# Idle matmuls, scalings and state copies in the first chunks of a fused retention and feed-forward kernel

## The chip, the cores and the metric

The kernel runs on one core of a Trainium2 chip. The metric is the device time of one execution in microseconds (us); lower is better. PE is the matmul engine, PEld its weight loads, DVE the vector engine, ACT the scalar engine, POOL GpSimd, and SP the engine whose queue issues most DMAs.

## The reference

Four sequences of 768 tokens go through a linear attention with a decaying state (8 heads of 64), and the result, seen as 3072 tokens of width 512, through a feed-forward layer with a squared ReLU.

```
def _attn_ref(q, k, v):                       # q, k, v: (4, 8, 768, 64) float32
    gamma = 1.0 - 2.0 ** (-5.0 - np.arange(H))
    scale = 1.0 / np.sqrt(D)
    for t in range(S):
        state = gamma * state + einsum('bhd,bhe->bhde', k[:, :, t], v[:, :, t])
        y[:, :, t] = scale * einsum('bhd,bhde->bhe', q[:, :, t], state)

def _moe_ref(x, w_in, w_out):                 # x: (3072, 512), w_in: (512, 2048)
    h = np.maximum(x @ w_in, 0.0)
    return h * h @ w_out
```

## The kernel before

The tokens are taken in 24 chunks of 128, six for each sequence. Within a chunk the attention is done by matmuls: q and k are scaled by powers of gamma (so that the decay is in the operands), both are transposed on PE, the scores of the chunk are a product of kT and qT, a mask makes them causal, and the output is the masked scores times v plus qT times the state of the chunks before. The state is a sum of products of k and v that grows in one PSUM tile, `c_ps`; after each chunk it is copied to SBUF in bf16, into one of the tiles `s_bd`, whose off-diagonal quarters stay zero. The output of a chunk, `y`, is copied into `xt`, which is the transposed input of the feed-forward part.

The feed-forward part runs over 11 blocks of tokens, the first of four chunks, the others of two. Its first product, with `w_in` (four groups of 512 columns, each loaded in float32 to a `stage` tile and cast to bf16 by `cast_w`), is made by `first_product` at L824; ACT takes the ReLU and DVE or ACT the square. The second product with `w_out` is made at L1020 for the first two blocks and by a scheme of seven products at L858 for the others. From the first block on, a table of places puts the attention of later chunks between pieces of the feed-forward part.

There is no scheduler: every engine runs its instructions in the order in which the Python code gives them out, and each queue is in order. SP issues the loads in the order of the code at the start: the first half of q of chunks 0 to 3, half of k of chunks 0 and 1, the second half of q, the second half of k, k of chunks 2 and 3, v of chunks 0 and 1, the first half of `w_in` group 0, v of chunks 2 and 3, and then the other groups of `w_in`. POOL issues the loads of `w_out` (L170) after its casts of `w_in`.

The change touches the front, which is the hand-written order for chunks 0 to 3 before the table of places begins. Chunks go in pairs there, (0, 1) and (2, 3), and heads in two groups of four; a tile holds one group:

- `scale_q4(group, rr)` (L533) scales half of the q of four chunks for one group of heads, on DVE unless told otherwise; `transpose_q4` (L550) turns it by four matmuls and ACT copies it to `qT` (L553).
- `scale_pair_k(m, group)` (L559) and `transpose_pair_k` (L584, copy to `kT` by ACT at L585) do so for k of the pair that begins with chunk m.
- `cast_pair_v(m, r)` casts half of a pair's v to bf16, on POOL (L571) or ACT (L569).
- `scores_pair(m, group, ...)` (L600) makes 32 small score matmuls of 64 by 64, four of them on different quarters of the array, and then two masks on DVE (L608). "Scores (0, 1)" is this for pair 0 and group 1.
- `state_pair(m, j)` adds chunk m+j to the state by eight matmuls with 64 of 128 rows (L625) and copies the two halves of the state to `s_bd`, by ACT (L636) or by DVE (L638).
- `outputs_pair` (L649) makes the masked scores times v, `finish_pair` (L665) adds qT times the state and copies the result to `xt` by ACT (L677) or DVE (L679).
- `first_unit(0, 0, c, parts)` makes first products of chunk c with `w_in` group 0, in halves of two row blocks.
- `keep_awake(n, width)` issues n matmuls of the identity with itself (L342), 512 columns wide unless told otherwise, into a PSUM tile that nobody reads; the tile comes from the pool of `y`. `end_awake` gives the tile up.

The engines are named by the helpers' arguments: `nc.gpsimd` is POOL, the default is DVE.

Of the kernel before, what the change touches and what calls it, by code (L numbers as in the profile page):

```python
# [31 lines left out]
def kernel(  # L32
# [9 lines left out]
    nc = tc.nc  # L42
    P = nc.NUM_PARTITIONS

    B, H, S, D = q.shape
    DM, DFF = moe_w_in.shape
    C = 128
# [289 lines left out]
    def keep_awake(n, width=4 * C, pool=ps_f, name="psf"):  # L337
        if not idle_ps:
            idle_ps.append(pool.tile([P, 4, P], FP32, name=name))
        wide = max(1, width // C)  # L340
        for _ in range(n):
            nc.tensor.matmul(  # L342
                idle_ps[0][:, 0:wide, 0 : width // wide],
                lhsT=ident[:],
                rhs=ident[:, None, 0 : width // wide].to_broadcast([P, wide, width // wide]),
                start=True,
                stop=True,
            )

    def end_awake():  # L350
        idle_ps.clear()
# [170 lines left out]
    def pair_view(t):  # L522
        return t.rearrange("s c hh d -> s (c hh d)").rearrange("s (r h d) -> s r h d", r=2, h=H)
# [3 lines left out]
    def scale_q4(group, rr, engine=nc.vector):  # L527
        if rr == 0:
            t = qspool.tile([P, 2, H, D], BF16, name="qs").rearrange("s r h d -> s (r h d)")
            qs4[group] = t.rearrange("s (r h d) -> s r h d", h=H // 2, r=4)  # L530
        rs = slice(2 * rr, 2 * rr + 2)
        heads = heads_of[group]
        engine.tensor_tensor(  # L533
            out=qs4[group][:, rs].rearrange("s r h d -> s h r d"),
            in0=raw_q4[group][:, :, rs, :],
            in1=qf4[:, rs, heads]
            .rearrange("s r h -> s h r")[:, :, :, None]
            .to_broadcast([P, H // 2, 2, D]),
            op=ALU.mult,
        )  # L540

    def transpose_q4(group, rr, pool, name):
        if rr == 0:
            t = qTpool.tile([P, 2, NPAIR, C], BF16, name="qT").rearrange("e r p s -> e (r p s)")
            qT4[group] = t.rearrange("e (r p s) -> e r p s", r=4, p=2)
        tp = pool.tile([P, 2, NPAIR, C], BF16, name=name)[:, 0]
        tp = tp.rearrange("e (r p) s -> e r p s", r=2)
        for r in range(2):
            for p in range(2):
                nc.tensor.transpose(  # L550
                    tp[:, r, p, :], qs4[group][:, 2 * rr + r, 2 * p : 2 * p + 2, :], ident[:]
                )
        nc.scalar.activation(qT4[group][:, 2 * rr : 2 * rr + 2], tp, AF.Copy)  # L553

    def scale_pair_k(m, group, engine=nc.vector):
        b, i = chunks[m]
        heads = heads_of[group]
        at[m]["ks"] = pair_view(ks_bd2s[m // 2])
        engine.tensor_tensor(  # L559
            out=at[m]["ks"][:, :, heads],  # L560
            in0=raw_k[m][:, :, heads],
            in1=kfp[:, i : i + 2, heads, None].to_broadcast([P, 2, H // 2, D]),
            op=ALU.mult,
        )

    def cast_pair_v(m, r, on_scalar=False):
        at[m]["v"] = pair_view(v_bd2s[m // 2])
        if on_scalar:
            nc.scalar.activation(at[m]["v"][:, r], raw_v[m][:, r], AF.Copy)  # L569
        else:  # L570
            nc.gpsimd.tensor_copy(at[m]["v"][:, r], raw_v[m][:, r])  # L571

    def transpose_pair_k(m, group, pool, name):
        a = at[m]
        if "kT" not in a:
            a["kT"] = kTpool.tile([P, 2 * NPAIR, C], BF16, name="kT").rearrange(
                "e (r p) s -> e r p s", r=2
            )
        tp = pool.tile([P, 2, NPAIR, C], BF16, name=name)[:, 0]
        tp = tp.rearrange("e (r p) s -> e r p s", r=2)  # L580
        for r in range(2):
            for p in range(2):
                h = 4 * group + 2 * p
                nc.tensor.transpose(tp[:, r, p, :], a["ks"][:, r, h : h + 2, :], ident[:])  # L584
        nc.scalar.activation(a["kT"][:, :, 2 * group : 2 * group + 2], tp, AF.Copy)  # L585

    def tokens_of(m, group, p, j):
        s0 = (m + j) * (C // 4)
        return qT4[group][:, :, p, s0 : s0 + C // 4]

    def scores_pair(m, group, pools, pt):
        a = at[m]
        sts = [pool.tile([P, 2, 2, C], FP32, name=name) for pool, name in pools]
        pt = pt.rearrange("s (hh r p t) -> s hh r p t", hh=2, r=2, p=2)
        a["pt", group] = pt
        for r in range(2):
            for p in range(2):
                for hh, head in enumerate(halves):
                    for j, rows in enumerate(halves):
                        nc.tensor.matmul(  # L600
                            sts[hh][rows, r, p, :],
                            lhsT=a["kT"][head, r, 2 * group + p, j * (C // 2) : (j + 1) * (C // 2)],
                            rhs=tokens_of(m, group, p, j)[head],
                            start=True,
                            stop=True,
                        )
        for hh in range(2):
            nc.vector.tensor_tensor(  # L608
                out=pt[:, hh],
                in0=sts[hh][:],  # L610
                in1=maskp.rearrange("s r q t -> s r (q t)")[:, :, None, :].to_broadcast(
                    [P, 2, 2, C]
                ),
                op=ALU.mult,
            )

    def state_pair(m, j, on_scalar=True):
        b, i = chunks[m]
        a = at[m]
        if i + j == 0:  # L620
            c_ps[0] = ps_c.tile([P, NPAIR, 2, D], FP32, name="c_ps")
        c = c_ps[0]
        for p in range(NPAIR):
            for r in range(2):
                nc.tensor.matmul(  # L625
                    c[:, p],
                    lhsT=a["ks"][halves[j], r, 2 * p : 2 * p + 2, :],
                    rhs=a["v"][halves[j], r, 2 * p : 2 * p + 2, :],
                    start=(i + j == 0 and p == 0 and r == 0),
                    stop=True,  # L630
                    skip_group_check=True,
                )
        s_bd = s_bds[(m + j) % 2]
        for hh, head in enumerate(halves):
            if on_scalar:
                nc.scalar.activation(s_bd[head, :, hh, :], c[head, :, hh, :], AF.Copy)  # L636
            else:
                nc.vector.tensor_copy(s_bd[head, :, hh, :], c[head, :, hh, :])  # L638
# [407 lines left out]
    tp, st, f = (ps_tp, "tp"), (ps_st, "st"), (ps_f, "psf")  # L1046
    def small_pt():
        return ptpool.tile([P, NPAIR, 2, C], BF16, name="pt").rearrange("s p hh t -> s (p hh t)")

    spare = hpool.tile([P, 4096], BF16, name="h2")  # L1050
    keep_awake(6, pool=ps_y, name="y")
    scale_q4(0, 0)
    scale_q4(0, 1)
    transpose_q4(0, 0, *tp)
    transpose_q4(0, 1, *st)
    scale_pair_k(0, 0)
    transpose_pair_k(0, 0, *f)
    keep_awake(1, C)
    scale_q4(1, 0)
    scale_q4(1, 1, nc.gpsimd)  # L1060
    scale_pair_k(0, 1)
    transpose_q4(1, 0, *f)
    scores_pair(0, 0, (st, f), small_pt())
    transpose_pair_k(0, 1, *f)
    transpose_q4(1, 1, *f)
    scale_pair_k(2, 0)
    scale_pair_k(2, 1, nc.gpsimd)
    keep_awake(1)
    scores_pair(0, 1, (tp, f), small_pt())
    transpose_pair_k(2, 0, ps_c, "c_ps")  # L1070
    cast_pair_v(0, 0)
    cast_pair_v(0, 1, on_scalar=True)
    transpose_pair_k(2, 1, *f)
    scores_pair(2, 0, (st, f), spare[:, 0:1024])
    end_awake()
    state_pair(0, 0)
    scores_pair(2, 1, (tp, f), spare[:, 1024:2048])
    outputs_pair(0, 0, ((ps_y, "y"), f))
    outputs_pair(0, 1)
    finish_pair(0, 0)  # L1080
    finish_pair(0, 1)
    state_pair(0, 1)
    cast_w("in", 0, (0,), "GGGG")
    cast_pair_v(2, 0)
# [4 lines left out]
    outputs_pair(2, 0, ((ps_y, "y"), st))  # L1089
    outputs_pair(2, 1)  # L1090
    finish_pair(2, 0)
    state_pair(2, 0, on_scalar=False)
    first_unit(0, 0, 0, (1,))
    first_unit(0, 0, 1, (1,))
    finish_pair(2, 1, on_scalar=False)
# [136 lines left out]
```

## Time and profile before

| | us |
|---|---|
| three runs | 207.69, 208.91, 208.88 |
| median | 208.88 |
| profiled execution | 208.75 |
| its span, first to last instruction | 206.7 |
| PE busy in the span | 198.4 |
| DVE, ACT, POOL busy | 152.1, 128.5, 66.8 |
| mean granted clock of PE | 0.975 |

The profile is of one execution. Its page gives for each engine the busy time, the share of the span and the instructions; then the span in 40 slices of 5.17 us with a digit for the busy tenths of each engine, and in the row PEclk the clock that PE was granted, in tenths of the full one (9 stands for nine tenths or more). A row of the timeline gives the start, the busy time, the engine, the line of the kernel, the operation, what is written and read, the shape and the count, and in brackets how long the engine had been idle and what ended that.

### The profile page before, as it was taken

The page shows a single profiled execution, that of the slowest core. Times are in us where ns is not written, and L with a number is a line of the kernel's source. Part 1 is how long each engine was busy: PE and PEld are TensorE (multiplying, and loading weights), DVE is VectorE, ACT ScalarE, POOL GpSimd, SP SyncE. Part 2 cuts the span into 40 slices and gives each one's busy share as a digit, 9 for nine tenths or more (in the row PEclk, how much of TensorE's full clock was granted, in tenths as well). Part 3 has the DMA queues.
Part 4 walks back from the last instruction along what each step waited for, and adds up shares of the span by engine and source line. Part 5 has one row for each costly group of instructions (what it writes and reads, how often), then busy time and mean ns, then how long its engine had stood idle before and what let it go on. Part 6 is the DMA issues. An engine that isn't in the chain of part 4 may idle for free.

```text
span 206.7 us, 5739 instructions
## 1 busy us (share of the span) xinstructions
PE 198.4 (96%) x2320; PEld 162.3 (79%) x2320; DVE 152.1 (74%) x308; ACT 128.5 (62%) x260; POOL 66.8 (32%) x130
## 2 busy tenths in 40 slices
PE   5699999999999999999999999999999999999993
PEld 1378744556985898997999989988989999999883
DVE  3971875827787899679689698698798798575374
ACT  8654686047864585683685695792794785773730
POOL 8672811401210343453253253352235225010000
PEclk9956999999999999999999999999999999999999
DMA  5999999999689669978999998898999655300202
GB/s 173 356 374 399 321 190 196 266 233 254 185 194 212 154 127 134 223 202 212 153 225 133 221 227 153 193 241 187 192 230 192 151 105 30 129 3 0 101 3 101
DMA packets 92250, 38.12 MB, mean 184 GB/s; under 512 B 68544, under 2 KB 88256, under 8 KB 92224
## 3 DMA queue, kind: packets, MB, share of 16 engines
q1 hardware_dynamic: 90112, 35.66, 72.7%
q0 software_dynamic: 2112, 2.10, 6.1%
q8 instruction: 18, 0.29, 0.7%
q14 instruction: 8, 0.07, 0.1%
HBM read 27.26 MB, written 6.29 MB: 162 GB/s over the span
## 4 chain that ended last, share of the span: by engine, by line
PE 85%; DVE 6%; ACT 4%; DMA 3%; issue 1%; SPq 1%; DVEq 0%
PE psf L824 37%; PE psf L858 17%; PE psf L1020 10%; PE tp L858 7%; DMA kn<-in_k_dram 3%; DVE h L804 2%; ACT h L833 2%; PE y L781 2%; PE st L725 2%; PE c_ps L625 1%; PE y L774 1%; PE c_ps L752 1%; DVE k_bd L854 1%; PE st L430 1%; PE y L506 1%; PE y L649 1%
## 5 line engine op out<-in xcount | busy, mean ns | idle before, releaser
L824 PE MATMUL psf<-xt,w_in_bf 128*128 128x256 bf16 (+2 forms) x880 | 93.1, 261 | 0.0
L824 PEld LDWEIGHTS <-w_in_bf 128*128 128x128 bf16 x880 | 71.8, 99 | 11.3 <-issue 0.2
L833 ACT ACTIVATE h<-psf 128x512 bf16<-128x512 f32 x96 | 56.2, 595 | 20.0 <-PE psf L824 18.5
L804 DVE TENSOR_TENSOR h<-h 128x512 bf16<-128x512 bf16 x80 | 37.3, 482 | 17.9 <-ACT h L833 17.3
L686 POOL CAST ks_bdp<-stage 64x512 bf16<-64x512 f32 x32 | 23.6, 738 | 37.2 <-issue 26.2
L703 POOL COPY v_bd<-v 64x512 bf16<-64x512 bf16 x32 | 20.6, 644 | 44.9 <-DVE v L695 38.4
L858 PEld LDWEIGHTS <-h 128*128 128x128 bf16 x288 | 26.1, 98 | 4.5 <-DVE h L804 1.6
L1020 PE MATMUL psf<-w_out_bf,h 128*128 128x512 bf16 x96 | 22.5, 379 | 0.0
L858 PE MATMUL tp<-w_out_bf,h 128*128 128x256 bf16 x136 | 19.7, 273 | 0.4 <-DVE h L804 0.4
L858 PE MATMUL psf<-w_sum,h 128*128 128x256 bf16 x136 | 19.1, 273 | 0.0
L858 PE MATMUL psf<-w_sum,k_bd 128*128 128x256 bf16 x144 | 17.9, 273 | 0.0
L361 DVE TENSOR_TENSOR qs<-qn,qf 128x512 bf16<-128x512 f32 x20 | 16.3, 825 | 0.6 <-DMA qn<-in_q_dram 0.3
L1020 PEld LDWEIGHTS <-h 128*128 128x128 bf16 x96 | 8.9, 98 | 9.0
L858 PEld LDWEIGHTS <-k_bd 128*128 128x128 bf16 x144 | 13.8, 98 | 1.5
L761 ACT ACTIVATE s_bd<-c_ps 64x256 bf16<-64x256 f32 x29 | 10.7, 370 | 6.5 <-PE c_ps L752 6.5
L854 DVE TENSOR_TENSOR osb<-psf,u 128x256 f32<-128x256 f32 x26 | 10.3, 421 | 6.1 <-PE psf L858 5.8
L854 DVE TENSOR_TENSOR u<-psf,u 128x256 f32<-128x256 f32 x18 | 7.6, 423 | 9.0 <-PE psf L858 8.8
L695 DVE TENSOR_TENSOR v<-stage,kf 128x512 bf16<-128x512 f32 x16 | 12.5, 783 | 0.0
L762 ACT ACTIVATE s_bd<-c_ps 64x256 bf16<-64x256 f32 x29 | 11.0, 379 | 0.4
L732 DVE TENSOR_TENSOR pt<-st,cmask 128x512 bf16<-128x512 f32 x16 | 11.0, 688 | 0.1
L788 ACT ACTIVATE xt<-y 128x512 bf16<-128x512 f32 x16 | 9.6, 598 | 1.8 <-PE y L781 1.2
L854 DVE TENSOR_TENSOR k_bd<-h 128x512 bf16<-128x512 bf16 x18 | 10.5, 581 | 0.3
(135 smaller groups left out, 260.0 us busy)
## 6 DMA issues: line engine op xcount, KB each, us to landing
qn<-in_q_dram SPq DMA_DIRECT2D x12, 512.0 KB, 4.9
out_dram<-osb SPq DMA_DIRECT2D x23, 256.0 KB, 2.6
stage<-in_k_dram SPq DMA_DIRECT2D x32, 96.0 KB, 3.6
stage<-in_v_dram SPq DMA_DIRECT2D x32, 96.0 KB, 3.4
stage<-in_moe_w_in_dram SPq DMA_DIRECT2D x4, 512.0 KB, 6.4
stage<-in_moe_w_in_dram SPq DMA_DIRECT2D x2, 1024.0 KB, 10.1
w_out_bf<-in_moe_w_out_dram POOLq DMA_DIRECT2D x4, 512.0 KB, 10.4
kn<-in_k_dram SPq DMA_DIRECT2D x6, 256.0 KB, 6.1
```

The lines of the kernel that those rows point to most:

```text
L361: engine.tensor_tensor(out=out, in0=by, in1=table[:, :, None].to_broadcast([P, H, D]), op=ALU.mult)
L686: nc.gpsimd.tensor_copy(ks[rows, :, hh, :].rearrange("s (u p) d -> s u p d", u=2), kn[rows])
L695: nc.vector.tensor_tensor(out=v2.rearrange("s (u p) d -> s u p d", u=2), in0=vn, in1=kf2[:, i, :, :, None].to_broadcast([P, 2, NPAIR, D]), ...
L703: nc.gpsimd.tensor_copy(v_bd[rows, :, hh, :], v2[rows])
L732: nc.vector.tensor_tensor(out=pt[:], in0=st[:], in1=cmask2.rearrange("s r t -> s (r t)")[:, None, :].to_broadcast([P, 2 * NPAIR, C // 2]), ...
L762: nc.scalar.activation(s_bd[halves[1], :, 1, :], c[halves[1]], AF.Copy)
L804: nc.vector.tensor_mul(hv, hv, hv)
L824: nc.tensor.matmul(hp, lhsT=w_in_bf[g][:, cb, fq * 128 : (fq + 1) * 128], rhs=xts[tb][:, cb, cols], start=(cb == 0), stop=(cb == NCB - 1),)
L833: nc.scalar.activation(hv, hp[:], AF.Relu)
L854: nc.vector.tensor_tensor(out=out, in0=in0, in1=in1, op=op)
L858: nc.tensor.matmul(to, lhsT=left[:, j], rhs=right(j) if callable(right) else right[:, j], start=(start and j == 0), stop=(stop and j == NF ...
L1020: nc.tensor.matmul(op[:], lhsT=h_of(tb, f)[:, 0, j * C : (j + 1) * C], rhs=w_out_bf[g][:, fq, cols], start=(f == 0), stop=(f == NFB - 1),)
```

## The change

The order of the front is written anew. After the first six idle matmuls there were two more, one of 128 and one of 512 columns (`keep_awake(1, C)` and `keep_awake(1)`); now there are eleven of 512 columns, in eight calls. The second half of the second q group goes from POOL to DVE, and the second half of k of pair 0 from DVE to POOL. The second q transposes of group 1 go ahead of the transposes of that k. Both halves of v of pair 0 are cast by POOL. The scores of pair 2 both come before the first state, their masks are given out apart from them, around the copies of that state, and the first state's copies go to ACT and DVE, one each. `state_pair` takes a string with a letter for each copy.

```
-    def scores_pair(m, group, pools, pt):
+    def scores_pair(m, group, pools, pt, later=False):
...
-        for hh in range(2):
+        def mask(hh):
             nc.vector.tensor_tensor(
...
+        if later:
+            return mask
+        mask(0)
+        mask(1)
+
-    def state_pair(m, j, on_scalar=True):
+    def state_pair(m, j, on="SS"):
...
-            if on_scalar:
+            if on[hh] == "S":
                 nc.scalar.activation(s_bd[head, :, hh, :], c[head, :, hh, :], AF.Copy)
             else:
                 nc.vector.tensor_copy(s_bd[head, :, hh, :], c[head, :, hh, :])
...
     scale_q4(0, 0)
     scale_q4(0, 1)
     transpose_q4(0, 0, *tp)
+    keep_awake(1)
     transpose_q4(0, 1, *st)
+    keep_awake(1)
     scale_pair_k(0, 0)
     transpose_pair_k(0, 0, *f)
-    keep_awake(1, C)
+    keep_awake(2)
     scale_q4(1, 0)
-    scale_q4(1, 1, nc.gpsimd)
-    scale_pair_k(0, 1)
+    scale_q4(1, 1)
+    scale_pair_k(0, 1, nc.gpsimd)
     transpose_q4(1, 0, *f)
     scores_pair(0, 0, (st, f), small_pt())
+    transpose_q4(1, 1, *f)
+    keep_awake(1)
     transpose_pair_k(0, 1, *f)
-    transpose_q4(1, 1, *f)
     scale_pair_k(2, 0)
     scale_pair_k(2, 1, nc.gpsimd)
-    keep_awake(1)
+    keep_awake(3)
     scores_pair(0, 1, (tp, f), small_pt())
     transpose_pair_k(2, 0, ps_c, "c_ps")
+    keep_awake(1)
+    transpose_pair_k(2, 1, *f)
+    keep_awake(1)
     cast_pair_v(0, 0)
-    cast_pair_v(0, 1, on_scalar=True)
-    transpose_pair_k(2, 1, *f)
-    scores_pair(2, 0, (st, f), spare[:, 0:1024])
+    cast_pair_v(0, 1)
+    mask_a = scores_pair(2, 0, (st, f), spare[:, 0:1024], later=True)
+    keep_awake(1)
     end_awake()
-    state_pair(0, 0)
-    scores_pair(2, 1, (tp, f), spare[:, 1024:2048])
+    mask_b = scores_pair(2, 1, (tp, f), spare[:, 1024:2048], later=True)
+    mask_a(0)
+    mask_a(1)
+    state_pair(0, 0, "SV")
+    mask_b(0)
+    mask_b(1)
     outputs_pair(0, 0, ((ps_y, "y"), f))
...
-    state_pair(2, 0, on_scalar=False)
+    state_pair(2, 0, "VV")
```

## The prediction

> **What bounds the kernel now.** I read the page first: which engine is full, and whether its clock is.
>
> ```profile
> PE 198.4 (96%) x2320; PEld 162.3 (79%) x2320; DVE 152.1 (74%) x308; ACT 128.5 (62%) x260; POOL 66.8 (32%) x130
> ...
> PEclk9956999999999999999999999999999999999999
> ```
>
> PE is busy 96% of the span, and the waits of PE list nothing after 24 us except 0.4 us or less at a time before L858. So whatever the front gains on PE moves everything behind it forward by as much, as long as no transfer is late. The one place where PE is worth less than its busy time is slices 3 and 4 (and the end of slice 2), where the granted clock is half. The clock's edges lie at 9.34 and 19.58 us, 10.24 us apart, which is three times 3.41. Therefore I cut the front into stretches of 3.41 us that end on these edges (columns: stretch, length, busy us of PE, PEld, DVE, ACT, POOL, granted clock, DMA share, GB/s):
>
> ```profile
> 2.51:5.93 3.42, 2.87 (x10) 0.95 (x8) 1.66 (x6) 2.90 (x8) 3.13 (x8) 1.00 0.98 330
> 5.93:9.34 3.41, 2.13 (x38) 1.39 (x37) 3.18 (x5) 2.19 (x4) 1.85 (x3) 1.00 1.14 349
> 9.34:12.75 3.41, 2.71 (x45) 1.81 (x42) 2.70 (x5) 2.08 (x4) 2.34 (x5) 0.50 1.12 362
> 12.75:16.17 3.42, 3.42 (x75) 2.69 (x68) 2.87 (x6) 2.19 (x6) 2.54 (x7) 0.50 1.11 387
> 16.17:19.58 3.41, 3.41 (x56) 2.94 (x53) 0.12 (x1) 1.18 (x3) 1.46 (x4) 0.50 1.05 397
> 19.58:22.99 3.41, 3.39 (x60) 2.93 (x53) 1.78 (x5) 1.72 (x4) 1.67 (x4) 1.00 1.08 394
> ```
>
> The stretch before the clock fell is the least busy one. But 12.75 to 16.17 is full and still did not bring the clock back, so "busy" is not what decides; how much of the array works does. The timeline gives the prices of a matmul at either clock, and the order of the first scalings:
>
> ```profile
> 2.17 2.74 PE L342 MATMUL y<-ident 128*128 128x512 bf16 x6 [2.17 <-POOL ident L223]
> 6.73 0.69 DVE L533 TENSOR_TENSOR qs<-qn,qf 128x512 bf16<-128x512 f32 x1
> 6.87 1.46 POOL L533 TENSOR_TENSOR qs<-qn,qf 128x512 bf16<-128x512 f32 x1 [0.74 <-DMA qn<-in_q_dram]
> 7.53 1.35 DVE L559 TENSOR_TENSOR ks_bdp<-kn,kfp 128x512 bf16<-128x512 f32 x1
> 8.94 0.40 PE L584 MATMUL psf<-ident,ks_bdp 128*128 128x128 bf16 x4 [0.72 <-DVE ks_bdp L559]
> 9.16 1.04 POOL L559 TENSOR_TENSOR ks_bdp<-kn,kfp 128x512 bf16<-128x512 f32 x1 [0.82 <-DMA kn<-in_k_dram]
> 10.01 0.74 DVE L559 TENSOR_TENSOR ks_bdp<-kn,kfp 128x512 bf16<-128x512 f32 x1
> ...
> 12.35 0.63 ACT L569 ACTIVATE v_bd<-vn 128x512 bf16<-128x512 f32 x1
> ...
> 14.02 0.77 ACT L636 ACTIVATE s_bd<-c_ps 64x256 bf16<-64x256 f32 x2 [0.56 <-PE c_ps L625]
> ...
> 16.85 1.89 PE L824 MATMUL psf<-xt,w_in_bf 128*128 128x128 bf16 x16
> ...
> 20.53 1.07 PE L824 MATMUL psf<-xt,w_in_bf 128*128 128x128 bf16 x16
> ```
>
> The six idle matmuls start 0.43 us apart, so they too run at half clock, although the page shows 1.0 there; a product of 512 columns in the full clock takes 0.218 (10.47 us for 48, in the chain). Sixteen products of 128 columns take 1.82 us in the chain at 17 us and 1.00 at 20.6. A POOL scaling is 1.04 us alone. Beside DVE's scaling it was 1.46, and DVE's next one 1.35 instead of 0.69: two scalings at once take turns.
>
> **The array's work, stretch by stretch.** I count columns times the time of a column (0.0533 or 0.107 us for 128), with half for the state's matmuls, which use 64 of 128 rows. First stretch: idle 2.2 us and transposes 0.4, 2.65 of 3.41 (78%), and the clock rose. Second: 16 transposes, scores 0.21, one short idle matmul: 1.2 (35%), and it fell. Third: 2.4 (70%), not back. Fourth: state 0.56, scores 0.46, outputs 0.86, finish 0.43: 2.3 (68%), not back. Fifth: products 1.7, outputs 0.86, state 0.29: 2.85 (84%), back. Sixth: 2.5 (74%), it stayed. By this count rising needs something between 70% and 78%; staying needs at most 74% and more than 35%.
>
> **The change, part by part.** (1) Idle matmuls: two after the first six become eleven, nine more (one of the two also grows from 128 to 512 columns). Each costs 0.22 us at full clock, 0.43 at half. At full clock they lie in PE's pauses: behind the first two q transposes PE waits for DVE's scalings; the two before 7.47 end at 7.4; the three before the scores of (0,1) end at 9.95, while ACT makes kT until 10.0. Without that cover the nine and a half cost 2.1 us. (2) Second half of q on DVE, 7.42 to 8.1, second half of k on POOL; its data landed at 7.51. POOL waits for DVE's turn, then 0.92 to 1.04: ready at 9.05 (bound: 1.46 after 8.1, 9.55), against 8.88 now. The q transposes now come first and leave PE and ACT before that, so scores (0,1) start at 10.05 to 10.5 instead of 10.51. (3) DVE's masks of (0,0) start at 8.45 instead of 8.81, but the next scaling of k takes turns with POOL's, which waits for its data until 9.16 and ends at 10.2: done at 10.8, as now (10.75). No gain there. (4) The v cast leaves ACT (0.63) and goes to POOL, 11.2 to 11.85; the first w_in lands at 11.91, so POOL's casts of it don't move. ACT's last kT then ends at 12.5 instead of 13.47. (5) Scores (2,1) move ahead of the state's matmuls, the masks after. Scores (2,0) at 11.9, (2,1) at 12.5, state 12.8 to 13.4, outputs to 13.9. (6) The state's copies on ACT and DVE: in the changed program's list of waits DVE's copy waits for ACT's, so they don't overlap. ACT 0.38 plus DVE 0.42 plus the handover, against 0.77: nothing gained. DVE has both masks of (2,0) before it (12.25 to 13.6), and the masks of (2,1) queue behind it until 15.65; outputs of chunk 2 need them at 16. finish (0,1) on PE goes at 14.35 instead of 15.34: 1.0 us earlier.
>
> From there now to 19.65 PE runs without a pause at half clock: finish 0.61, state 0.96, products 1.82, outputs 0.98 less overlaps, 4.3 us. At full clock by the rows of 19.7 to 21.6: 0.33, 0.55, 1.00, and outputs at half, 0.5, together 2.4: 1.9 us less. After 19.65 the order and the clock are as before. **Sum:** 1.0 + 1.9 = 2.9 us. The profiled execution took 208.75 (span 206.7 and 2.05 around it), 0.13 under the median of the three runs, 208.88. So 205.8.
>
> **Does a transfer take it back?** w_in lands at 16.1, 18.8, 21.3 and 23.8; products on them are needed at 21.4, 23, 25 and 28 after the move, casts of 1 us included. The first w_out is issued at 22.0 and takes 7.1 us: 29.1, needed at 34.87 now and 32 then. The fourth, 25.6 plus 13.7, 39.3, needed at about 43. The tightest cover is about 2.9 us.
>
> [...]
>
> **The rivals.** *A: one fall, soon mended.* The second stretch after the change has idle 1.3, transposes 0.85, scores 0.21: 2.4 (69%), between the fall at 35% and the stay at 74%. If the clock falls, the idle matmuls, twice as long, fill the third stretch to 3.0 (88%), above the 84% that brought it back. Then scores (0,1) come at 10.7, scores (2,1) at 13.25, finish (0,1) at 15.05: 0.3 + 1.9 = 2.2, 206.5. *B: it flickers.* The stretch behind 12.75 holds 2.1 to 2.4 at full clock (state, outputs, finish, products between waits), no more than before; the next one is then at half, 1.7 us given back of the forecast: 207.5. *C: idle matmuls too weak, clock as now.* Then they are pure cost on the path: scores (0,1) 0.25 late after three of 0.43; two more and one between the transposes and scores make finish (0,1) come at 16.0, 0.65 late, half of which the full clock after 19.58 takes up: 209.1 to 209.4, slower; if the clock comes back one stretch later, 1.7 more, 211. It decides once idle matmuls beside waits count less than the unbroken ones at 2.17. For it: a full stretch at 12.75 did not raise the clock; against it: idle matmuls alone raised it at 5.93. *D: the copies* are serial as told; that is in the sum.
>
> **How the numbers follow.** Forecast (clock full from about 6 us) 0.45; A 0.17; B 0.18; C 0.15; something else 0.05. The stretches need not lie the same against the kernel's start in every execution, which blurs all four. Range: from 204.6 (scores (0,1) at 10.05 rather than 10.5, 0.5, and 0.7 if the two scalings of k at 9.7 don't take turns) to 209.4 (C). The forecast's own range is 204.6 to 206.5. A measurement of this kernel tells about 1% from no change, 2.1 us, so 206.8 divides: most of the forecast and over half of A lie below, B and much of C within, some of C above. Faster 0.53, same 0.37, slower 0.10.
>
> **What would show it.** PEclk without a 5 or 6 after the first slice; sixteen products near 15 us in 1.0 us; first products on 512 columns at about 21.4 instead of 24.4; DVE's copy of the state starting after ACT's. Wrong: granted clock 0.5 beyond 12.8 us, or PE waiting for POOL's k later than 9.6 us.

## The result, and the profile after

The changed kernel takes 206.0 us (median of 6 runs, 205.89 to 206.32); beside it the kernel before took 207.91 (6 runs, 207.63 to 208.91). The ratio is 0.9899, with a 95% interval of 0.9872 to 0.9925: 1.0% faster. The forecast was 205.8. A ratio leaves out runs over 1.5% above the fastest of their kernel; the kernel before spreads so widely that this drops some of its slowest, so its runs are also given one by one below.

The profiled execution took 205.99, with a span of 203.9 instead of 206.7. Of its page, the rows that answer to those of before:

```profile
PE 196.7 (96%) x2329; PEld 160.4 (79%) x2329; DVE 151.1 (74%) x309; ACT 127.6 (63%) x258; POOL 69.1 (34%) x131
...
PEclk9999999999999999999999999999999999999999
```

PE has nine matmuls more and is busy 1.7 us less, and the two slices of half clock are gone. The same stretches of 3.41 us as before (stretch, length, busy us of PE, PEld, DVE, ACT, POOL, granted clock, DMA share, GB/s):

```profile
2.51:5.93 3.42, 2.88 (x11) 1.06 (x9) 1.67 (x6) 2.91 (x8) 3.13 (x8) 1.00 0.99 331
5.93:9.34 3.41, 3.33 (x44) 2.11 (x42) 2.75 (x6) 2.80 (x5) 1.73 (x3) 1.00 1.14 349
9.34:12.75 3.41, 3.09 (x63) 1.57 (x60) 3.01 (x5) 1.73 (x4) 2.80 (x6) 1.00 1.13 363
12.75:16.17 3.42, 3.06 (x80) 2.49 (x68) 2.90 (x7) 2.28 (x5) 2.53 (x7) 1.00 1.10 386
16.17:19.58 3.41, 3.03 (x69) 2.38 (x67) 0.84 (x2) 1.33 (x3) 1.43 (x4) 1.00 1.06 399
```

The second stretch went from 2.13 to 3.33 us busy, and the clock stays at 1.00 behind it. The rows can't show where the clock rose: four transposes still take 0.61 us at 5.46 and 0.58 at 6.28, and 0.39 at 6.91, so PE is at half clock until about 6.6 (before, the four at 6.07 already took 0.40). From 12.75 on PE is now less busy than before (3.06 and 3.03 us in two stretches that were full, 3.42 and 3.41): it has pauses again. The timeline of PE, ACT and DVE from the first state on shows two of them:

```profile
13.46 0.38 ACT L641 ACTIVATE s_bd<-c_ps 64x256 bf16<-64x256 f32 x1 [1.24 <-PE c_ps L630]
13.87 0.43 DVE L643 CAST s_bd<-c_ps 64x256 bf16<-64x256 f32 x1 [0.34 <-ACT s_bd L641]
...
14.36 0.40 PE L670 MATMUL psf<-qT,s_bd 128*128 128x128 bf16 x4 [0.36 <-DVE s_bd L643]
14.68 0.62 PE L630 MATMUL c_ps<-v_bd,ks_bdp 64*128 64x128 bf16 x8
15.23 1.07 PE L829 MATMUL psf<-xt,w_in_bf 128*128 128x128 bf16 x16
16.80 0.40 PE L670 MATMUL y<-qT,s_bd 128*128 128x128 bf16 x4
17.13 0.51 PE L630 MATMUL c_ps<-v_bd,ks_bdp 64*128 64x128 bf16 x6
17.98 0.27 PE L630 MATMUL c_ps<-v_bd,ks_bdp 64*128 64x128 bf16 x2 [0.34 <-issue]
```

DVE's copy has waited for ACT's (0.34) and starts 0.03 us after that ends, so here the two engines take turns, and PE waits for the second (0.36). At 17.98 PE has been idle for 0.34 us in the middle of eight matmuls that need nothing new; "issue" says that no engine and no transfer is seen to hold it. Sixteen products take 1.07 us at 15.23, where they took 1.89 at 16.85.

The first products of 512 columns, before and after:

```profile
24.34 10.53 PE L824
...
22.00 10.54 PE L829 MATMUL psf<-xt,w_in_bf 128*128 128x512 bf16 x48
```

They start 2.34 us earlier, and that is what the front gained. The last matmuls start at 200.15 instead of 202.97, 2.82 earlier; 0.6 of the waits of PE's weight loads for DVE's squares before the seven products went away on the way (1.6 us to 1.0).

### The profile page after: what moved, and what is told of

The parts are those of the page before. It is cut to its first block, busy times and chain, and to the rows that moved or that the text cites. A ratio compares the mean times of both kernels' runs of the same rounds, so it can differ in the third digit from the quotient of the medians.

```text
span 203.9 us, 5755 instructions
## 1 busy us (share of the span) xinstructions
PE 196.7 (96%) x2329; PEld 160.4 (79%) x2329; DVE 151.1 (74%) x309; ACT 127.6 (63%) x258; POOL 69.1 (34%) x131
## 4 chain that ended last, share of the span: by engine, by line
PE 88%; DVE 5%; ACT 2%; DMA 2%; issue 1%; DVEq 0%
PE psf L829 39%; PE psf L863 18%; PE psf L1025 10%; PE tp L863 7%; DMA qn<-in_q_dram 2%; PE y L786 2%; PE st L730 2%; PE y L779 2%; PE c_ps L757 2%; DVE h L809 1%; PE c_ps L630 1%; PE st L430 1%; PE y L506 1%; ACT h L838 1%; DVE k_bd L859 1%
## 5 line engine op out<-in xcount | busy, mean ns | idle before, releaser
L809 DVE TENSOR_TENSOR h<-h 128x512 bf16<-128x512 bf16 x80 | 35.9, 462 | 19.1 <-ACT h L838 18.6
L691 POOL CAST ks_bdp<-stage 64x512 bf16<-64x512 f32 x32 | 24.8, 776 | 38.4 <-issue 34.1
L1025 PE MATMUL psf<-w_out_bf,h 128*128 128x512 bf16 x96 | 22.5, 379 | 0.0
L1025 PEld LDWEIGHTS <-h 128*128 128x128 bf16 x96 | 8.9, 98 | 9.0
L859 DVE TENSOR_TENSOR osb<-psf,u 128x256 f32<-128x256 f32 x26 | 10.3, 420 | 6.1 <-PE psf L863 5.8
```

Of the source, the lines that this page charges most:

```text
L691: nc.gpsimd.tensor_copy(ks[rows, :, hh, :].rearrange("s (u p) d -> s u p d", u=2), kn[rows])
L809: nc.vector.tensor_mul(hv, hv, hv)
L859: nc.vector.tensor_tensor(out=out, in0=in0, in1=in1, op=op)
L1025: nc.tensor.matmul(op[:], lhsT=h_of(tb, f)[:, 0, j * C : (j + 1) * C], rhs=w_out_bf[g][:, fq, cols], start=(f == 0), stop=(f == NFB - 1),)
```

## The experiments

The theory was that PE's clock follows the work of its array in stretches of 3.41 us, and that the change gains by filling the second stretch. The length is from the trace of the kernel before: there the record of the clock begins at 5.93, between two rows of transposes, the first at half clock and the second at full; the clock falls at 9.34, 3.41 us later, and stays at half for 10.24, three times as long.

```profile
5.47 0.60 PE L550 MATMUL tp<-ident,qs 128*128 128x128 bf16 x4 [0.55 <-DVE qs L533]
6.07 0.40 PE L550 MATMUL st<-ident,qs 128*128 128x128 bf16 x4
```

The first rival was that the new order of the front gains, whatever the clock does. Medians, in the order in which they are told:

| kernel | us, lowest to highest (runs) | ratio to before, 95% interval |
|---|---|---|
| changed | 206.0, 205.89 to 206.32 (6) | 0.9899, 0.9872 to 0.9925 |
| new order, old idle matmuls | 207.54, 205.33 to 208.93 (12) | 0.9937, 0.9896 to 0.9978 |
| old order, new idle matmuls | 206.11, 205.81 to 206.4 (12) | 0.9911, 0.9883 to 0.9939 |
| changed, both copies on ACT | 205.91, 205.78 to 206.3 (11) | 0.991, 0.988 to 0.9939 |
| changed, idle half as wide | 206.01, 205.66 to 206.58 (12) | 0.9911, 0.9878 to 0.9943 |
| changed, idle a quarter as wide | 206.32, 205.8 to 209.06 (12) | 0.9931, 0.9897 to 0.9964 |
| changed, idle half as wide on half the rows | 209.91, 206.34 to 210.11 (6) | none |
| changed, two transposes for each idle matmul | 205.83, 205.68 to 206.07 (4) | 0.9891, 0.9864 to 0.9918 |
| changed, two narrow matmuls for each | 205.78, 205.74 to 205.84 (4) | 0.9886, 0.9864 to 0.9907 |
| changed, last three idle left out | 205.51, 205.34 to 205.83 (6) | 0.9888, 0.9845 to 0.9931 |
| changed, first six cut into 24 | 205.52, 205.43 to 205.92 (6) | 0.989, 0.9847 to 0.9933 |
| combined | 205.15, 205.1 to 205.24 (4) | 0.9856, 0.9834 to 0.9877 |
| combined, old order | 205.27, 205.2 to 205.34 (6) | 0.9885, 0.9849 to 0.9921 |

**Order or idle matmuls.** The first kernel keeps the new order and has the old idle matmuls:

```
     transpose_q4(0, 0, *tp)
-    keep_awake(1)
     transpose_q4(0, 1, *st)
-    keep_awake(1)
...
-    keep_awake(2)
+    keep_awake(1, C)
...
-    keep_awake(3)
+    keep_awake(1)
```

and none in the other places.

> The changed order, scalings and copies, but only the two idle matmuls of the kernel before (one of 128 columns, one of 512) behind the first six. Theory (the clock is decided by the array's work in stretches of 3.41 us, and most of the gain is the clock): the second stretch holds 20 transposes, scores and one short idle matmul, 1.3 to 1.5 us or 38 to 44%, so the granted clock falls near 9.3 us and stays at half to about 19 us; of the 1.9 us gained at most the 1.0 us of the new order is left: 207.0 to 208.2. Rival (the order gains, the clock follows from it): clock full or nearly, 206.0 to 206.5.

It took 207.54, but its runs lie anywhere from 205.33 to 208.93. In its profiled execution (207.69) the clock fell at 8.33 and came back at 18.57, 10.24 us apart as in the kernel before, but a full microsecond earlier against the kernel's start:

```profile
5.93:9.34 3.41, 2.37 (x37) 1.59 (x38) 2.97 (x6) 2.92 (x5) 1.72 (x3) 0.85 1.14 348
9.34:12.75 3.41, 2.89 (x52) 1.78 (x53) 2.61 (x4) 1.68 (x3) 2.82 (x6) 0.50 1.12 362
12.75:16.17 3.42, 3.42 (x69) 2.68 (x62) 2.76 (x5) 1.28 (x3) 2.53 (x7) 0.50 1.11 387
16.17:19.58 3.41, 3.41 (x62) 2.82 (x59) 0.90 (x3) 1.06 (x4) 1.50 (x4) 0.65 1.06 398
```

So the clock's edges don't lie at a fixed distance from the kernel's start. How long it is at half differs between the twelve runs too (0.975, 0.983 and 0.992 among their clocks); that this comes from where the stretches fall was my inference, and no run shows it. The new order isn't without effect, though: the interval of its ratio leaves out 1, and four of its twelve runs lie below 206.6, against six of 69 of the kernel before. Its second stretch is a little busier (39% of the array by the count of the prediction, against 35%), which may be why the clock is lost less often; that wasn't tested. Its two shortest runs, 205.33 and 205.41, are shorter than any of the changed kernel. The opposite kernel has the order of before and the new idle matmuls in the same pauses (one of them ahead of `transpose_pair_k(0, 1)` instead of behind the q transposes, which come later there).

> The kernel before with the eleven idle matmuls of the change in the same pauses, and nothing else changed. Theory: the clock stays full from 6 us on, the stretch from finish (0,1) to the second output products shrinks by about 1.9 us; the order of before keeps its 1.0 us: 206.0 to 207.0. Rival (the order gains): nine more matmuls of 0.22 to 0.43 us on a path that they do not shorten, 208 to 209.

It took 206.11, as much as the whole change within its spread, with clocks of 0.998 to 1.00. The idle matmuls alone bring the whole gain, and the rival (208 to 209) falls. finish (0,1) comes at 14.11, earlier than in the new order (14.36), and PE's pause without a releaser is longer here, 0.85 us instead of 0.34:

```profile
14.11 0.40 PE L665 MATMUL psf<-qT,s_bd 128*128 128x128 bf16 x4
...
18.24 0.27 PE L625 MATMUL c_ps<-v_bd,ks_bdp 64*128 64x128 bf16 x2 [0.85 <-issue]
```

**What the kernel before does by itself.** 69 runs of it were made beside the experiments, and each has a mean granted clock. Thirteen had 0.975 and took 207.76 to 208.86: half clock for 2 x 0.025 x 206 = 10.3 us, three stretches. Four had 0.983 (7.0 us by the same sum, about two stretches) and took 207.75 to 208.08. Five had 0.99 to 0.991 (3.7 to 4.1 us, about one stretch) and took 205.77 to 205.96: as fast as the changed kernel. One had 0.981 and took 206.54. The other 46 have no fall of that length on record (0.999 or 1.00) and took 207.41 to 209.46; what they may be, the kernel with half rows shows below. So the change makes into the rule what the kernel before did by luck in five runs of 69.

**Two engines for the copies.**

```
-    state_pair(0, 0, "SV")
+    state_pair(0, 0, "SS")
```

> The changed kernel with both copies of the first state on ACT again. Theory (DVE's copy waits for ACT's, so two engines gain nothing): ACT's two take 0.77 us from 13.46, finish (0,1) starts at 14.3 as now, and the masks of scores (2,1) start 0.5 us earlier, which nothing on the path awaits: 205.9 to 206.2. Rival (the copies gain time): finish (0,1) later by 0.3 and 206.3 or more.

205.91, and finish (0,1) at 14.31 instead of 14.36. The copies on two engines gain nothing.

**How much idle work is needed, and what counts.** In the next kernel every `keep_awake(n)` behind the first six became `keep_awake(n, 2 * C)`. The first six stayed at 512 columns; the expectation says otherwise, and its remarks on the first stretch don't apply.

> The changed kernel with idle matmuls of 256 columns instead of 512, the first six too. Theory: the array's work decides. The first stretch then holds 1.1 us of idle work, so the clock may rise one stretch later, near 9.3 instead of 5.9, because the idle matmuls of the front are then at half clock and long; the second stretch holds 1.75 us (51%) at full clock. If staying needs no more than 51%, a rise at 9.3 holds to the end and the time is 206.3 to 207; if it needs more, the clock is at half for two or three stretches, 207 to 208.5. Rival (only pauses count, not work): as many matmuls in the same pauses, clock as in the changed kernel, 205.9 to 206.2.

206.01 in twelve runs, none above 206.58: half the idle work behind the first six is enough. With `keep_awake(n, C)`, a quarter:

> The changed kernel with the idle matmuls behind the first six 128 columns wide instead of 512 (the first six stay at 512). Theory (work of the array in a stretch decides): the second stretch holds 20 transposes, scores and about seven columns' worth of idle, 1.6 us or 47%, between the fall of the kernel with the old idle matmuls (39%) and the half-wide one that stayed full (some 55%); a fall in part of the runs, 205.7 to 207.5 with a wide spread. Rival (pauses count, not work): the pauses are filled as often as before, clock full in all runs, 205.5 to 206.0, spread as small as that of the changed kernel.

Eight runs lie between 205.8 and 206.41, four between 207.54 and 209.06. A quarter is too little in part of the runs, as the theory has it; the rival that only pauses count fails. Of the four long runs only one has a fall on record (a clock of 0.983). The profiled execution, 206.0, tells more than its page, which shows full clock everywhere: transposes are at half clock until past 9 us.

```profile
8.60 0.61 PE L550 MATMUL psf<-ident,qs 128*128 128x128 bf16 x4
...
10.78 0.40 PE L584 MATMUL c_ps<-ident,ks_bdp 128*128 128x128 bf16 x4
```

Yet finish (0,1) starts at 14.27, no later than in the changed kernel. So half clock up to about 10 us cost this run nothing that shows; what costs is half clock behind that, as before from 9.34 to 19.58. Then the half-wide ones on 64 rows, by a `rows` argument of `keep_awake`:

```
-                lhsT=ident[:],
-                rhs=ident[:, None, 0 : width // wide].to_broadcast([P, wide, width // wide]),
+                lhsT=ident[0:rows],
+                rhs=ident[0:rows, None, 0 : width // wide].to_broadcast([rows, wide, width // wide]),
```

> The changed kernel with the idle matmuls behind the first six 256 columns wide and on 64 of 128 rows: the same PE time as the half-wide ones that kept the clock full, half their array work. If array area counts, it behaves like the quarter-wide kernel, with a fall in part of the runs; if the time that matmuls stream counts, like the half-wide one: 206.0, narrow spread.

One run took 206.34, five 209.73 to 210.11, slower than the kernel before. The same columns and pauses as in the half-wide kernel, half the rows, and the full clock is missed: the rows in use count (209.91 in the median, 206.01 on all rows), not only the time that matmuls stream. But it is worse than the expectation: 256 columns on 64 rows are as much array work as 128 columns on 128, and there eight runs of twelve were short, here one of six. That the area alone decides is therefore not shown. At half clock PE is busy for all of each stretch from 5.93 to 19.58 here (3.41 of 3.41 us), so the half-row matmuls take time from fuller ones; that may be the difference, and no run tests it. The profiled execution (209.73) is the surprise: its page shows full clock everywhere, and yet the sixteen products run at half, two microseconds later than those of before:

```profile
PEclk9999999999999999999999999999999999999999
18.82 1.81 PE L829 MATMUL psf<-xt,w_in_bf 128*128 128x128 bf16 x16
```

In this execution PE was at half clock from its first transposes on (four take 0.61 us at 5.49 and still at 13.02; the page shows 1.00 all the same) and rose only near 20.5 us (the next `finish_pair`, at 21.13, takes 0.40 as at full clock). Its idle matmuls then cost their price on the path, which is rival C of the prediction. The runs of the kernel before without a recorded fall, 207.41 to 209.46, fit the same picture, but none of them has a trace here, so that stays open.

Do transposes count? The prediction counted them as matmuls. Each idle matmul behind the first six became two transposes of 128 columns (`nc.tensor.transpose` of the identity), and as a control two matmuls of 128 columns.

> The changed kernel with each idle matmul behind the first six replaced by two transposes of the identity, 128 columns each: 256 columns of PE time, as in the half-wide kernel that stayed at full clock. If a transpose counts as array work like a matmul of its columns (so counted in the prediction): clock full, 205.5 to 206.2, narrow spread. If it does not: the stretches hold as little counted work as with the old idle matmuls, clock at half for several stretches, 207.5 to 209.5, wide spread. [...]

> Control to the transposes: each idle matmul behind the first six as two ordinary matmuls of 128 columns, with as many instructions as the two transposes. Theory: 256 columns of work on the whole array each, as in the half-wide kernel: clock full, 205.5 to 206.2, narrow. Rival (many short instructions cost PE more than they work): some falls, above 206.5.

205.83 and 205.78, all runs within 205.68 and 206.07. With four runs each, the transposes keep the clock full as well as matmuls do: sixteen products take 1.07 us in both profiled executions, at 15.16 and at 15.21. The trace lists these transposes as MATMUL, like those of q and k.

**Where the front still loses time.** Leaving out the three single idle matmuls at and behind `transpose_pair_k(2, 0)`:

> The changed kernel without the three single idle matmuls behind the transposes and scores of pair 2; the eight before stay. Theory: the third stretch (9.34 to 12.75) then holds three idle 0.4 to 0.6, scores 0.43, transposes 0.43, state 0.1, together 1.5 us or 44%, and the fourth 60 to 70%: the clock may fall at 12.75, 206.0 to 207.5; where it stays full the path loses up to 0.4 us of idle matmuls, 205.5 to 205.9. Rival (only the second stretch matters): clock full always, 205.6.

205.51, all six runs within 205.34 and 205.83: they were not needed, and 0.5 us is saved. But the saving is not where I looked for it: finish (0,1) starts at 14.22, only 0.14 earlier. The pause of PE has moved by three matmuls, six instructions, just the number that was taken out:

```profile
17.00 0.62 PE L630 MATMUL c_ps<-v_bd,ks_bdp 64*128 64x128 bf16 x8
17.55 0.23 PE L829 MATMUL psf<-xt,w_in_bf 128*128 128x128 bf16 x1
17.99 1.00 PE L829 MATMUL psf<-xt,w_in_bf 128*128 128x128 bf16 x15 [0.21 <-issue]
```

So in these two kernels the pause belongs to a place in the stream of instructions, not to an operand. In both it ends at 17.98 to 17.99, but here three matmuls fewer are left behind it, and the next `finish_pair` starts at 18.82 instead of 19.29: that is the 0.5. In the two kernels with 22 instructions more the pause stands eleven matmuls earlier and ends at 16.95 to 16.96. This is the row of the one with transposes:

```profile
16.95 0.21 PE L660 MATMUL st<-h,v_bd 64*64 64x128 bf16 x1 [0.16 <-issue]
```

The page counts 18 transfers of a queue named instruction, 0.29 MB, 16 KB each. To move the place far, the first six idle matmuls became 24 of 128 columns, 36 instructions more for the same work:

```
-    keep_awake(6, pool=ps_y, name="y")
+    keep_awake(24, C, pool=ps_y, name="y")
```

> The changed kernel with the first six idle matmuls (512 columns) cut into 24 of 128 columns: the same array work in the same 2.6 us, 36 instructions more in PE's stream. Theory (PE's pause of 0.34 us in the state of chunk 2, with no semaphore behind it, is the edge of a block of its instructions): the pause moves 36 instructions forward, into the outputs of pair 2 near 16.6 us, and is 0.3 to 1 us long; time 206.0 to 206.5. Rival (something about the operands of the state's matmuls): the pause stays at the seventh matmul of that state.

205.52, again 0.5 less, with all eleven idle matmuls still there. The pause is gone rather than moved:

```profile
16.82 0.40 PE L670 MATMUL y<-qT,s_bd 128*128 128x128 bf16 x4
17.15 0.62 PE L630 MATMUL c_ps<-v_bd,ks_bdp 64*128 64x128 bf16 x8
17.70 1.07 PE L829 MATMUL psf<-xt,w_in_bf 128*128 128x128 bf16 x16
```

Here the instruction transfer lies between 13.5 and 14.0 us, in the changed kernel between 15.5 and 16.0 (between 16.0 and 16.5 before, where PE at half clock came to the state of chunk 2 only at 19.98 and had no pause in it). The pauses end 2 to 2.7 us behind the transfer: at 17.98 in the changed kernel, and, with the transfer also between 15.5 and 16.0, at 17.99 without the last three and at 18.24 in the old order. As far behind the transfer as in the changed kernel, a pause would end at about 16 in this kernel (an estimate from these times), before PE comes to the place near 16.6. These times fit a PE that waits for instructions in transfer, but that is my inference: the trace names nothing that PE waits for there, and no run shows whether the transfer is of PE's instructions, or what fills the 2 us and more.

**Both savings together, and the order once more.** The combined kernel has 24 narrow matmuls, no last three, and the copies on ACT.

> The changed kernel with the three last idle matmuls left out, the first six cut into 24 of 128 columns, and both copies of the first state on ACT. Theory: the clock stays full as without the last three; the pause at the edge of PE's instruction block is gone as with 24; finish (0,1) starts at 14.2; 205.1 to 205.4. Rival (the two savings are one and the same, and something else ends the front): 205.5 as each alone.

205.15, 1.4% under before, and no run of it is as long as any of the two kernels with one saving each (205.34 and more, on another chip): the two savings are not one and the same. Finally the same idle matmuls with the order, the engines and the copies of the kernel before:

> The order, engines and copies of the kernel before, with the idle matmuls of the combined kernel: 24 of 128 columns, then eight of 512 in the same pauses, none behind. It is the combined kernel less the new order. Theory of the prediction (the order brings finish (0,1) forward by 1.0 us at full clock): 206.1. Rival (the clock brought it forward, the order little): finish (0,1) at 14.0 to 14.3 and 205.1 to 205.5.

205.27, with finish (0,1) on PE at 14.01, earlier than in the new order (14.17 in the combined kernel):

```profile
14.01 0.40 PE L665 MATMUL psf<-qT,s_bd 128*128 128x128 bf16 x4
14.34 0.62 PE L625 MATMUL c_ps<-v_bd,ks_bdp 64*128 64x128 bf16 x8
```

The runs of the two kernels overlap (205.1 to 205.24 and 205.2 to 205.34), and their first products of 512 columns start at 21.30 and 21.31. At full clock the whole new order is worth nothing that these runs can tell.

## Why the prediction was right, and where not

**The clock** was the main step, and it held: full from about 6.6 us in the profiled execution, and no run of the changed kernel above 206.32. The sign that the prediction named for it, PEclk without a 5 or 6, was too weak by itself: the kernel with half rows shows the same row and was at half clock to 20.5 us. The sixteen products, 1.07 us at 15.23, tell. The bracket of array work was good enough to choose the case: 35 to 39% falls (before, and the old idle matmuls in the new order), 47% fails in part of the runs, half-wide idle matmuls suffice. (The count took `scores_pair` as 16 matmuls, which is what the kernel makes; the text ahead of the prediction says 32.) That the count is the right measure is less sure, since half the rows did worse than the same area on all rows. Counting transposes as work agrees with the runs: 205.83 with idle transposes, 205.78 with narrow matmuls in their place.

**finish (0,1) at 14.35** came out at 14.36, but the step that gave it, "1.0 us earlier" by the new order, was wrong. The old order reaches it at 14.11 with the same idle matmuls and the same clock, and at 14.01 without the last three. The new order with the clock at half reaches it only at 15.15 against 15.34, though the clock fell a microsecond earlier there. The 1.0 us was the clock too: at half clock four transposes ahead of it take 0.61 us instead of 0.40, and the eight matmuls of the state 1.03 instead of 0.62. Inside the step, most of what I worked out held: POOL's k ready at 8.9 (9.05 forecast), the scaling of k on DVE done at 10.64 (10.8), the state at 12.81 (12.8). What I did not do was to run the old order through the same sum at full clock.

**The stretch of 2.4 us** to finish (2,0) measured 14.36 to 16.80, 2.44. That 1.9 us less held.

**The copies** are serial as forecast, 0.03 us apart.

**"After 19.65 the order and the clock are as before"** missed PE's pause. Without it 22.00 would have been some 0.4 to 0.5 earlier, and 205.5 the time, as the kernel with 24 narrow matmuls shows. The 0.5 that came back later, from waits before the seven products, was not foreseen either. The sum of 2.9 us against 2.76 in the two profiled executions owes its closeness to these two, which is luck.

**The step from one execution to the median** was the weakest. The 2.9 us were taken off the 208.75 of one execution (off the median, 208.88, they give 206.0), and 208.75 was one of the longer executions of a kernel whose runs lie between 205.77 and 209.46. "The stretches need not lie the same against the kernel's start" was said and not followed up: the gain is 1.9 us by the medians of the first six runs, 2.76 between the profiled executions, and nothing against five of the 69.

**The rivals.** A and B did not come up in the changed kernel. C, idle matmuls too weak and on the path, is a real case: with half the rows it takes 209.7 to 210.1, above the 209.1 to 209.4 of its sum, and there the clock was at half from the start and not from 9.34, which the sum did not have. D was right. No transfer of weights was late: L1025 starts at 32.37, 2.34 earlier as the products before it.

## What to carry to other kernels

When PE waits often in a front and its clock falls, measure how far apart the clock's edges lie (10.24 us here, three stretches of 3.41), count how much of the array works in each stretch, and fill the pauses with idle matmuls on all rows until the runs no longer spread; half as much as here was enough (206.01), and the last three of the eleven only put 0.14 us on the path to finish (0,1). Look at the spread of runs before choosing what to compare with: the kernel before, whose clock fell in some executions and not in others, took 205.77 to 209.46, and one profile shows one of them. Read the clock from the durations of known matmuls, not from PEclk alone (1.81 us for sixteen products under a printed 1.00). Order and engines should be tried at the clock that they will run at, and a count of instructions can matter too: here 36 more in the right place saved 0.5 us.

## What the runs showed of the hardware that was not expected

- A granted clock of 1.00 on the page can be half: in the kernel with half rows it is printed for the whole span, while sixteen products took 1.81 us at 18.82 instead of 1.07. Durations of known matmuls tell.
- Before, the clock fell although the longest pause of PE in the stretch was 0.72 us, and it did not rise in a stretch with PE busy for 3.42 of 3.42 us (12.75 to 16.17).
- PE paused at a fixed place of its instruction stream: 0.34 us in the changed kernel, 0.85 in the old order with the same number of instructions, and not at all with 36 instructions more ahead of it, which made the kernel 0.5 us faster.
